# One more block's output in seven half-size products, and one unit transposed by DMA instead of TensorE

## The chip, the cores and the metric

The kernel runs on one core of one Trainium2 chip. The metric is the device time of one execution in microseconds. In the profile, PE is TensorE's matmuls, PEld its weight loads, DVE is VectorE, ACT is ScalarE, POOL is GpSimd, SP (SyncE) the engine that issues the DMAs. The granted clock is the share of TensorE's full clock that it was allowed to run at; 1.0 is all of it.

## The reference

Attention in chunks of 64 tokens, then a bilinear feed-forward layer:

```python
# q, k, v: (8, 8, 576, 64); w_a, w_b: (512, 1536); w_out: (1536, 512)
scores = q_c @ k_c.T / sqrt(64)            # in each chunk of 64 tokens
attn   = softmax(scores);  out = attn @ v_c
x = out.transpose(0, 2, 1, 3).reshape(4608, 512)
return ((x @ w_a) * (x @ w_b)) @ w_out     # float32 (4608, 512)
```

## The kernel before

The 4608 tokens are 9 blocks (0 to 8) of 512, and each block is 2 units of 256. For a unit, q and k are loaded, cast to bf16 on GpSimd (unit 0's on VectorE), transposed, multiplied to scores, normalized, and multiplied with v to give `xT`. Then a block goes through the two feed-forward products (`ab`) and the output product.

From block 2 on, products are done by a seven-product scheme for 2x2 block matrices (Strassen-Winograd): seven half-size products in place of eight, at the price of sums. For the output the sums are `s1..s4` of the activations `ab` and `t1..t4` of the weights `w_out`. `combine_wo` and `combine_ab` make them, all on GpSimd:

```python
def combine_wo(part, j):                   # weight sums, third j of the rows of w_out
    ...
    o, x0, x1, op = ((t3, b22, b12, SUB), (t2, t3, b11, ADD),
                     (t4, b21, t2, SUB), (t1, b12, b11, SUB))[part]
    nc.gpsimd.tensor_tensor(out=o, in0=x0, in1=x1, op=op)

def combine_ab(K, part, j, eng=None):      # sums of block K's activations
    ...
    o, x0, x1, op = ((s1, a21, a22, ADD), (s2, s1, a11, SUB),
                     (a21, a11, a21, SUB), (s4, a12, s2, SUB))[part]
    (eng or nc.gpsimd).tensor_tensor(out=o, in0=x0, in1=x1, op=op)
```

Blocks 0 and 1 are different. While they run, attention still has to get ahead and the weights are still being summed. Block 0 is done plainly; block 1 plainly in two halves, `h(1)` being one step of it; and both outputs are plain products (`out_part`, matmuls of 512 columns). Every engine works through its own list in program order. The code that builds the lists:

```python
cast(4); cast(5); load(6)                  # units 0 to 5 are transposed on PE (PE_UNITS = 6)
...                                        # block 1, interleaved with attention:
bring(6); h(8); out_0(0); transpose_pe(4); h(2); scores(4); out_0(1); transpose_pe(5)
h(1); normalize(4); h(1); scores(5); h(1); values(4); bring(7); h(1)
normalize(5); out_0(2); values(5); combine_x(2); h(1); out_0(3)

for K in range(2, NBLK):
    for i in range(NWP):                   # group i of block K
        ...
        now.p1()
        if last: last.add7()               # VectorE: two additions, of C and u, v
        chunk(...)                         # a part of the previous block's output
        if last: last.p3()
        attend(K, i, 0); now.p6()
        if last: last.p4()                 # PE: product t4 into C, after add7
        ...
```

`bring(U)` casts unit U, loads the next one and transposes U by DMA. `add7` comes first in VectorE's list for each group, and PE cannot start product `p4` before it. Whatever stands in VectorE's list ahead of `add7` can stall PE.

The softmax here doesn't subtract the row's maximum and nothing guards it: scores larger than these inputs give would overflow.

Of the kernel before, what the change touches and what calls it, by code (L numbers as in the profile page):

```python
# [8 lines left out]


PE_UNITS = 6
AB_SCALE = 256.0
OUT_SCALE = 1.0 / AB_SCALE

# [2 lines left out]
def kernel(  # L17
# [10 lines left out]
    nc = tc.nc  # L28
# [48 lines left out]
    warm_in = consts.tile([128, 512], BF16)  # L77
# [33 lines left out]
    def cast_ab(i):  # L111
        for n in ("wb", "wa"):
            w_ab[n, i] = wpool.tile([128, NKT, WCOL], FP16, name=f"{n}{i}")
            nc.gpsimd.tensor_copy(out=w_ab[n, i], in_=staged.pop((n, i)))
# [31 lines left out]
            out=wo_sb[:, 2 * i:2 * i + 2], in_=staged.pop(("wo", i))  # L146
        )

    def combine_wo(part, j):
        k = slice(2 * j, 2 * j + 2)  # L150
        k2 = slice(HFT + 2 * j, HFT + 2 * j + 2)
        b11, b12 = wo_sb[:, k, 0:256], wo_sb[:, k, 256:512]
        b21, b22 = wo_sb[:, k2, 0:256], wo_sb[:, k2, 256:512]
        t1, t2, t3, t4 = [t[:, k] for t in wo_t]
        o, x0, x1, op = (
            (t3, b22, b12, SUB), (t2, t3, b11, ADD), (t4, b21, t2, SUB), (t1, b12, b11, SUB)
        )[part]
        nc.gpsimd.tensor_tensor(out=o, in0=x0, in1=x1, op=op)

    raw = {}  # L160

# [19 lines left out]
    def load(U, names="qkv"):  # L181

        for n in names if U < NU else "":
            src = {"q": q, "k": k, "v": v}[n]
            if U < PE_UNITS and n != "v":
                st = st_pool.tile([128, H, 2, D], FP32, name="st")
                for r, b, s, m in pieces(U):
                    nc.sync.dma_start(
                        out=st[r // 2:(r + m) // 2].rearrange("p h i d -> p h (i d)"),
                        in_=src[b, :, s:s + m, :].rearrange("h (p i) d -> p h (i d)", i=2),  # L190
                    )
                staged[n, U] = st.rearrange("p h i d -> p i h d")
            else:
                staged[n, U] = st_pool.tile([128, 2, H, D], FP32, name="st")
                load_natural(staged[n, U], src, U)

    def cast(U, names="qkv"):
        for n in names if U < NU else "":
            raw[n, U] = raw_pool.tile(
                [128, 2, H, D], BF16, name=f"{n}_raw"  # L200
            )
            eng = nc.vector if U == 0 and n != "v" else nc.gpsimd
            eng.tensor_copy(out=raw[n, U], in_=staged.pop((n, U)))  # L203


# [2 lines left out]
    def transpose_pe(U, names="qk"):  # L208
        if U not in qkt:
            qkt[U] = qkt_pool.tile([128, 2, 2, NKT, 128], BF16, name="qkt")  # L210
        for n in names:
            w = "qk".index(n)
            src = raw.pop((n, U))
            tp = bank().bitcast(BF16).rearrange("c (i m p) -> c i m p", i=2, m=NKT)
            for i in range(2):
                for m in range(NKT):
                    nc.tensor.transpose(
                        tp[:, i, m, :],
                        src[:, i, 2 * m:2 * m + 2, :].rearrange("p j d -> p (j d)"),
                        identity,  # L220
                    )
            dst = qkt[U][:, w].rearrange("c g m (p i) -> c i m g p", i=2)
            for i in range(2):
                cp = nc.vector.tensor_copy if w == 0 or U == 1 else nc.scalar.copy
                cp(out=dst[:, i], in_=tp[:, i].rearrange("c m (g p) -> c m g p", g=2))

    def transpose_dma(U):
# [12 lines left out]
    def scores(U):  # L240
        t = qkt.pop(U)
        E_of[U] = sm_pool.tile([128, 2, NKT, 2, 64], BF16, name="E")
        sc = [bank().rearrange("p (m g s) -> p m g s", m=NKT, g=2) for _ in range(2)]
        for m in range(NKT):
            for g in range(2):
                for j in range(2):
                    for cl in range(2):
                        nc.tensor.matmul(
                            sc[j][cl * 64:cl * 64 + 64, m, g, :],
                            t[j * 64:j * 64 + 64, 1, g, m, cl * 64:cl * 64 + 64],  # L250
                            t[j * 64:j * 64 + 64, 0, g, m, cl * 64:cl * 64 + 64],
                            start=True,
                            stop=True,
                        )
        for j in range(2):
            nc.scalar.activation(out=E_of[U][:, j], in_=sc[j], func=AF.Exp, scale=scale)
# [55 lines left out]
    def slot(s=None, f=None):  # L312

        if s is not None and s >= NU:
            s = None
        if f is not None:
            sums(f)
            inverse(f)
        if s is not None:
            scores(s)  # L320
        if f is not None:
            values(f)

    def bring(U):

        if U >= NU:
            return
        cast(U, "qk")
        load(U + 1, "q")
        if U < NU:  # L330
            transpose_dma(U)
        cast(U, "v")
        load(U + 1, "kv")
# [285 lines left out]
    with tc.manual_schedule(  # L619
# [22 lines left out]
        cast_ab(1)  # L642
        cast_ab(2)
        cast_ab(3)
        transpose_pe(1, "q")
        scores(0)
        transpose_pe(1, "k")
        sums(0, halves=None)
        keep_warm(2)
# [30 lines left out]
        for ft in range(NFT):  # L680
            ab_step(0, ft)
            if 3 <= ft < 10:
                combo()
            if ft == 6:
                transpose_pe(2)
            if ft == 8:
                slot(2)
            if ft == 10:
                slot(None, 2)

        cast(4)
        cast(5)
        load(6)

        outs = []

# [4 lines left out]
        def half(ft, u):  # L701
            ab_step(1, ft, 256 * u, 256 * u + 256)
            if ft > 9 if u == 0 else ft != 5 and ft != 9 and ft != 11:
                combo()
            if u == 1 and ft % 2 and ft > 2:
                combine_w(ft // 2 - 1, 3)

        halves = [(ft, u) for u in range(2) for ft in range(NFT)]

# [19 lines left out]
        h(2)  # L729
        values(3)  # L730
        bring(6)
        h(8)
        out_0(0)
        transpose_pe(4)
        h(2)
        scores(4)
        out_0(1)
        transpose_pe(5)
        h(1)
        normalize(4)  # L740
        h(1)
# [1 line left out]
        h(1)  # L743
        values(4)
        bring(7)
        h(1)
        spread[:] = [psum_a, psum_q]
        normalize(5)
        out_0(2)
        spread[:] = [psum_t]  # L750
        values(5)
        combine_x(2)
        h(1)
        out_0(3)
        assert not halves and not combos

# [21 lines left out]
        def attend(K, i, n):  # L778
            for f in attention.get((K, i, n), ()):
                f()  # L780

        wo_sums = [(p, j) for p in range(4) for j in range(3)]
        last = None
        chunks = {
            2: (0, 0, 1, 1, 1, 1, 1, 1, 1, 1, 1, 1),
            3: (1, 1, 2, 2, 1, 1, 2, 2, 1, 1, 1, 1),
            4: (1, 1, 1, 1, 1, 1, 2, 2, 1, 1, 1, 1),
            NBLK - 1: (1,) * 12,
        }
# [8 lines left out]
        for K in range(2, NBLK):  # L798
            for i in range(NWP):
                if i == 1:  # L800
                    if K == 2:
                        outs += [
                            lambda tg=tg, p=p: out_part(1, tg, p, (psum_o, psum_q)[tg % 2])
                            for tg in range(4) for p in range(3)
                        ]
                    else:
                        for j in range(3):
                            combine_ab(K - 1, 3, j)
                if i in (1, 3):
                    bring(2 * K + 4 if i == 1 else 2 * K + 5)  # L810
                if K == 2:
                    for _ in range(2 if i < 3 else 1):
                        combine_wo(*wo_sums.pop(0))
                if K == 3 and i == 1:
                    while wo_sums:
                        combine_wo(*wo_sums.pop(0))
                if K == 2 and i == 0:
                    combine_w(NWP - 1, 3)
                if K > 2 and i == 0:
                    g = OutGroup(K - 1)  # L820
                    outs += [
                        lambda g=g, n=n, th=th: g.part(n, th) for n in range(7) for th in range(2)
                    ]
                now = Group(K, i)
                now.p1()
                if last:
                    last.add7()
                chunk(chunks.get(K, chunks[4])[2 * i])
                if last:
                    last.p3()  # L830
                attend(K, i, 0)
                now.p6()
                if last:
                    last.p4()
                    finish(last)
                now.p2()
                chunk(chunks.get(K, chunks[4])[2 * i + 1])
                attend(K, i, 1)
                now.p5()
                now.p7()  # L840
                last = now
# [47 lines left out]
```

## Time and profile before

| | before |
|---|---|
| median time | 310.88 us (310.45 to 311.45) |
| span in the profile | 309.1 us |
| PE busy | 95% |
| GpSimd busy | 58% |

The page of the kernel before: the busy table, and rows of the table of 40 slices (7.7 us each, busy share in tenths).

```profile
PE 293.2 (95%) x3476; PEld 228.9 (74%) x3478; DVE 205.2 (66%) x342; ACT 194.0 (63%) x350; POOL 178.6 (58%) x168
...
PE   2879989999999999999999999999999999999995
...
POOL 0575656644538688936782777377737711780560
PEclk9999999999999999999999999999999999999999
```

PE is the limit. After the start its row is 9 nearly everywhere. GpSimd has room: 178.6 us busy of 309.

The view of what PE waited for (total us, times, longest):

```profile
PE pb L355 <- DVE xT L305: 1.7, 1, 1.7
PE pa L355 <- DVE xT L305: 1.5, 1, 1.5
PE pa L263 <- ACT v_sb L363: 0.5, 1, 0.5
```

Apart from the waits for the first casts (5.4, 0.8 and 0.5 us) these are the longest. Nothing after the start of block 1 is over 0.5 us. GpSimd's timeline around the end of block 1 (start us, us, engine, line, operation, output<-input, count, and idle time before it with what ended it):

```profile
64.36 1.04 POOL L203 CAST v_raw<-st 128x1024 bf16<-128x1024 f32 x1 [0.78 <-PE pt L217]
67.44 1.31 POOL L203 CAST q_raw<-st 128x1024 bf16<-128x1024 f32 x1 [2.04 <-DMA st<-in_q_dram]
69.98 1.04 POOL L203 CAST k_raw<-st 128x1024 bf16<-128x1024 f32 x1 [1.23 <-DMA st<-in_k_dram]
...
79.36 1.04 POOL L203 CAST k_raw<-st 128x1024 bf16<-128x1024 f32 x1 [4.29 <-DMA st<-in_k_dram]
...
95.37 3.37 POOL L158 TENSOR_TENSOR wot<-wot,wo 128x512 f16<-128x512 f16 x3
```

GpSimd idles for the DMA here, up to 4.3 us at a time. Three of its sums take 3.37 us (the last line). VectorE and PE at the start of block 2:

```profile
81.41 0.43 DVE L385 TENSOR_TENSOR s<-s,xT 128x512 f16<-128x512 f16 x1
...
87.67 0.69 DVE L443 TENSOR_TENSOR c_sb<-pc,v_sb 128x512 f32<-128x512 f32 x1 [1.74 <-ACT v_sb L416]
88.28 0.69 DVE L444 TENSOR_TENSOR pc<-pc,u_sb 128x512 f32<-128x512 f32 x1
```

```profile
88.34 0.60 PE L405 MATMUL pb<-s,t 128*128 128x256 f16 x4
89.02 0.60 PE L405 MATMUL pc<-xT,t 128*128 128x256 f16 x4
```

A VectorE sum (128x512, 16 bit) takes 0.43 us here. The two additions end at 88.97 us, and the `p4` product (`pc<-xT,t`) starts at 89.02 us.

### The profile page before, as it was taken

What the parts mean: (1) busy time and instruction counts of PE and PEld (TensorE: products, weight loads), DVE (VectorE), ACT (ScalarE), POOL (GpSimd) and SP (SyncE); (2) the same over time, 40 slices, a digit from 0 to 9 for tenths busy, and PEclk for the clock granted to TensorE, in tenths of its full rate; (3) what the DMA queues carried; (4) which work ended last, traced back from release to release, by engine and by line L of the source; (5) the groups of instructions that cost most, each with busy time, mean ns of one, the idle gap of its engine ahead of it and who ended that gap; (6) DMA issues with size and microseconds to landing.
All of it is one profiled execution on the core that took longest, in us unless ns stands there. A gap on an engine that the chain in (4) does not pass through costs nothing.

```text
span 309.1 us, 8485 instructions
## 1 busy us (share of the span) xinstructions
PE 293.2 (95%) x3476; PEld 228.9 (74%) x3478; DVE 205.2 (66%) x342; ACT 194.0 (63%) x350; POOL 178.6 (58%) x168
## 2 busy tenths in 40 slices
PE   2879989999999999999999999999999999999995
PEld 1534557866566768888888888888888888888884
DVE  3345663967866686567757776677668766965872
ACT  1643557448575657766877686768775867566531
POOL 0575656644538688936782777377737711780560
PEclk9999999999999999999999999999999999999999
DMA  7999999999989994698439943993493000300025
GB/s 233 303 382 279 274 326 344 246 228 200 272 209 221 222 240 120 91 251 220 125 70 244 241 130 86 215 293 94 102 174 134 6 0 2 136 3 3 0 77 197
DMA packets 138887, 54.03 MB, mean 175 GB/s; under 512 B 114016, under 2 KB 132960, under 8 KB 138848
## 3 DMA queue, kind: packets, MB, share of 16 engines
q1 hardware_dynamic: 138704, 53.36, 70.8%
q8 instruction: 27, 0.44, 0.6%
q10 hardware_dynamic: 144, 0.13, 0.1%
q14 instruction: 12, 0.10, 0.1%
HBM read 37.75 MB, written 9.44 MB: 153 GB/s over the span
## 4 chain that ended last, share of the span: by engine, by line
PE 81%; DVE 6%; ACT 4%; POOL 4%; issue 2%; DMA 2%; SPq 0%; DVEq 0%; POOLq 0%; ACTq 0%
PE pb L405 17%; PE pc L405 11%; PE pa L405 10%; PE po L541 9%; PE pq L541 8%; PE pb L609 3%; PE pb L355 3%; PE pc L355 3%; PE po L355 3%; DMA st<-in_q_dram 2%; PE pq L355 2%; POOL so L485 2%; PE pa L355 2%; PE pt L296 1%; PE pt L263 1%
## 5 line engine op out<-in xcount | busy, mean ns | idle before, releaser
L405 PEld LDWEIGHTS <-t 128*128 128x128 f16 x504 | 48.3, 98 | 9.9 <-issue 3.9
L443 DVE TENSOR_TENSOR c_sb<-pc,v_sb 128x512 f32<-128x512 f32 x42 | 28.8, 686 | 35.7 <-ACT v_sb L416 35.0
L485 POOL TENSOR_TENSOR so<-ab_sb 128x512 f16<-128x512 f16 x20 | 23.1, 1152 | 50.9 <-DVE ab_sb L455 50.9
L405 PE MATMUL pb<-s,wa 128*128 128x256 f16 x336 | 50.6, 273 | 0.1
L405 PE MATMUL pa<-xT,wb 128*128 128x256 f16 x336 | 50.4, 273 | 0.0
L416 ACT COPY u_sb<-pb 128x512 f32<-128x512 f32 x42 | 24.7, 587 | 24.8 <-PE pb L405 23.5
L541 PEld LDWEIGHTS <-ab_sb 128*128 128x128 f16 x336 | 32.9, 98 | 4.2 <-issue 0.4
L405 PEld LDWEIGHTS <-wb 128*128 128x128 f16 x336 | 32.9, 98 | 4.0
L405 PEld LDWEIGHTS <-wa 128*128 128x128 f16 x336 | 31.0, 98 | 6.2 <-issue 0.2
L203 POOL CAST k_raw<-st 128x1024 bf16<-128x1024 f32 x17 | 18.1, 1062 | 28.8 <-DMA st<-in_k_dram 28.8
L455 DVE SCALAR_TENSOR_TENSOR ab_sb<-pc,c_sb 128x512 f16<-128x512 f32 x42 | 28.9, 688 | 6.9 <-PE pc L405 5.5
L455 DVE SCALAR_TENSOR_TENSOR ab_sb<-pb,b_sb 128x512 f16<-128x512 f32 x42 | 28.8, 687 | 2.8 <-PE pb L405 2.4
L416 ACT COPY v_sb<-pb 128x512 f32<-128x512 f32 x42 | 24.9, 592 | 8.1 <-PE pb L405 8.1
L423 ACT COPY pb<-pa 128x512 f32<-128x512 f32 x42 | 24.6, 586 | 8.4 <-PE pa L405 8.3
L416 ACT COPY b_sb<-pa 128x512 f32<-128x512 f32 x42 | 25.0, 595 | 7.7 <-PE pa L405 7.7
L444 DVE TENSOR_TENSOR pc<-pc,u_sb 128x512 f32<-128x512 f32 x42 | 29.0, 689 | 0.0
L203 POOL CAST v_raw<-st 128x1024 bf16<-128x1024 f32 x18 | 19.2, 1065 | 15.6 <-DMA st<-in_v_dram 9.3
L305 DVE TENSOR_TENSOR xT<-pt,ln 128x512 f16<-128x512 f32 x30 | 19.4, 684 | 12.2 <-PE pt L296 12.2
L541 PEld LDWEIGHTS <-so 128*128 128x128 f16 x252 | 24.6, 98 | 3.4 <-issue 0.5
L203 POOL CAST q_raw<-st 128x1024 bf16<-128x1024 f32 x17 | 17.9, 1056 | 13.4 <-DMA st<-in_q_dram 12.8
L405 PE MATMUL pb<-s,t 128*128 128x256 f16 x168 | 25.3, 273 | 0.4 <-ACT pb L423 0.4
L405 PE MATMUL pc<-s,t 128*128 128x256 f16 x168 | 25.2, 272 | 0.5 <-DVE ab_sb L455 0.5
(132 smaller groups left out, 578.9 us busy)
## 6 DMA issues: line engine op xcount, KB each, us to landing
out_dram<-o_sb SPq DMA_DIRECT2D x34, 256.0 KB, 3.4
st<-in_v_dram SPq DMA_DIRECT2D x32, 256.0 KB, 4.2
st<-in_q_dram SPq DMA_DIRECT2D x23, 256.0 KB, 4.8
st<-in_k_dram SPq DMA_DIRECT2D x23, 256.0 KB, 3.5
st<-in_moe_w_b_dram SPq DMA_DIRECT2D x6, 512.0 KB, 8.0
st<-in_moe_w_a_dram SPq DMA_DIRECT2D x6, 512.0 KB, 8.0
st<-in_moe_w_out_dram SPq DMA_DIRECT2D x6, 512.0 KB, 6.7
st<-in_q_dram SPq DMA_DIRECT2D x4, 512.0 KB, 5.6
```

The costliest lines, as they stand in the source:

```text
L203: eng.tensor_copy(out=raw[n, U], in_=staged.pop((n, U)))
L305: nc.vector.tensor_tensor(out=x.rearrange("p m (g c s) -> p m g c s", g=2, c=2)[:, :, :, cl, :], in0=av[cl], in1=rs[:, cl].rearrange("p m ...
L355: nc.tensor.matmul(ps[n], w_ab[n, i][:, kt, o:o + 128], xT[:, kt, c0:c1], start=(kt == 0), stop=(kt == NKT - 1),)
L405: nc.tensor.matmul(t[:, h * 256:h * 256 + 256], w[:, kt, h * 128:h * 128 + 128], x[:, kt], start=start and h == 0 and kt == 0, stop=h == 1 ...
L416: nc.scalar.copy(out=t, in_=src)
L423: nc.scalar.copy(out=self.B, in_=self.A)
L443: nc.vector.tensor_tensor(out=self.c, in0=self.C, in1=self.v, op=ADD)
L444: nc.vector.tensor_tensor(out=self.C, in0=self.C, in1=self.u, op=ADD)
L455: nc.vector.scalar_tensor_tensor(out=self.dst[:, :, c0:c0 + 256], in0=t.rearrange("p (h n) -> p h n", h=2), scalar=AB_SCALE, in1=o.rearran ...
L485: (eng or nc.gpsimd).tensor_tensor(out=o, in0=x0, in1=x1, op=op)
L541: nc.tensor.matmul(t[:, c0:c0 + 256], a[:, kt, th * 128:th * 128 + 128], w[:, kt], start=n in (0, 4) and first and kt == 0, stop=last and ...
L609: nc.tensor.matmul(out_ps[K, tg], ab_tiles[K][:, ft, tg * 128:tg * 128 + 128], wo_sb[:, ft], start=(ft == 0), stop=(ft == NFT - 1),)
```

## The change

The intent: block 1's output in seven products as well, which spares PE work; unit 5 transposed by DMA (`PE_UNITS = 5`, `bring(5)`), which spares PE its 16 transposes; and smaller moves at the start. The sums that this needs are brought forward: `t3, t2, t4` and block 1's `s1, s2, s3` to GpSimd during block 1, and `t1` and `s4` to VectorE at the start of group 1 of block 2, ahead of its `add7`.

```diff
-PE_UNITS = 6
+PE_UNITS = 5
@@ cast
-            eng = nc.vector if U == 0 and n != "v" else nc.gpsimd
+            eng = nc.vector if (n, U) in (("q", 0), ("k", 0), ("k", 1)) else nc.gpsimd
@@ transpose_pe: evictions
-                cp = nc.vector.tensor_copy if w == 0 or U == 1 else nc.scalar.copy
+                dve = i == 0 if U == 0 or (U, w) == (1, 0) else w == 0 or U == 1
+                cp = nc.vector.tensor_copy if dve else nc.scalar.copy
@@ start
+        scores(0)
         transpose_pe(1, "q")
-        scores(0)
@@ block 0
+            if ft == 9:
+                sums(2)
+                inverse(2)
             if ft == 10:
-                slot(None, 2)
+                values(2)
@@ block 1
+        def combine_wo_all(part, eng=None):
+            for j in range(3):
+                combine_wo(part, j, eng)
         cast(4)
-        cast(5)
-        load(6)
+        bring(5)
+        combine_wo_all(0)
@@ half
+            if u == 1 and ft % 2 and ft > 6:
+                for part in range(3):
+                    combine_ab(1, part, ft // 2 - 3)
@@
         bring(6)
+        combine_wo_all(1)
@@
-        transpose_pe(5)
@@
         bring(7)
+        combine_wo_all(2)
         h(1)
-        spread[:] = [psum_a, psum_q]
+        spread[:] = [psum_q, psum_o]
         normalize(5)
@@
+        whole = bank(psum_q)
+        nc.tensor.matmul(whole, warm_in[:, :128], warm_in, start=True, stop=True)
         out_0(3)
@@ blocks 2 to 8: parts of the previous block's output in each half group
-            2: (0, 0, 1, 1, 1, 1, 1, 1, 1, 1, 1, 1),
-            3: (1, 1, 2, 2, 1, 1, 2, 2, 1, 1, 1, 1),
@@
                 if i == 1:
                     if K == 2:
-                        outs += [... out_part(1, tg, p, ...) ...]   # cut
-                    else:
-                        for j in range(3):
-                            combine_ab(K - 1, 3, j)
+                        combine_wo_all(3, nc.vector)
+                    for j in range(3):
+                        combine_ab(K - 1, 3, j, nc.vector if K == 2 else None)
-                (the weight sums spread over blocks 2 and 3)
-                if K > 2 and i == 0:
+                if i == 0:
                     g = OutGroup(K - 1)
```

More of the change, by code (lines that the diff above doesn't have):

```diff
@@ L147, in cast_wo, with combine_wo @@
         )
-    def combine_wo(part, j):
+    def combine_wo(part, j, eng=None):
         k = slice(2 * j, 2 * j + 2)
@@ L157, in combine_wo @@
         )[part]
-        nc.gpsimd.tensor_tensor(out=o, in0=x0, in1=x1, op=op)
+        (eng or nc.gpsimd).tensor_tensor(out=o, in0=x0, in1=x1, op=op)
     raw = {}
@@ L780, in attend @@
                 f()
-        wo_sums = [(p, j) for p in range(4) for j in range(3)]
         last = None
         chunks = {
[2 rows of a table removed]
             4: (1, 1, 1, 1, 1, 1, 2, 2, 1, 1, 1, 1),
@@ L801 @@
                     if K == 2:
-                        outs += [
-                            lambda tg=tg, p=p: out_part(1, tg, p, (psum_o, psum_q)[tg % 2])
-                            for tg in range(4) for p in range(3)
-                        ]
-                    else:
-                        for j in range(3):
-                            combine_ab(K - 1, 3, j)
+                        combine_wo_all(3, nc.vector)
+                    for j in range(3):
+                        combine_ab(K - 1, 3, j, nc.vector if K == 2 else None)
                 if i in (1, 3):
                     bring(2 * K + 4 if i == 1 else 2 * K + 5)
-                if K == 2:
-                    for _ in range(2 if i < 3 else 1):
-                        combine_wo(*wo_sums.pop(0))
-                if K == 3 and i == 1:
-                    while wo_sums:
-                        combine_wo(*wo_sums.pop(0))
                 if K == 2 and i == 0:
                     combine_w(NWP - 1, 3)
-                if K > 2 and i == 0:
+                if i == 0:
                     g = OutGroup(K - 1)
```

## The prediction

> **What bounds the kernel now.** TensorE: busy 95% of the 309.1 us span (busy table), 81% of the last chain. From 136 us on the windows show it busy almost without a gap; only the first 136 us can give much back. It waits there (view of waits) 5.4 us for the first cast, 0.8 and 0.5 for unit 1's casts, 1.7 at 17.1 us (unit 1's xT), 1.5 at 42.0 us (unit 2's xT), 0.5 at 75.5 us (bank of the sums of unit 5), 0.4 at 84 us, 0.3 at 131 us (GpSimd's output-weight sums).
>
> **What TensorE saves.**
> - Block 1's output: 48 matmuls of 512 columns (12 groups of 0.86 us) become 84 of 256 columns (14 groups of 0.655 us): -1.2.
> - Unit 5's 16 PE transposes (69.45 to 70.34 us): -0.9.
> - Prologue (split evictions, scores(0) earlier, unit 1's k cast on VectorE, 0.69 against 1.04 us): -0.6.
> - Unit 2's sums one step earlier, but ScalarE's b_sb copy then sits behind ln and exp (2.1 us): -0.5 of the 1.5 us.
> - Other banks for sums(5): -0.5; waits at 84 and 131 us: -0.5.
> - New whole-bank matmul that waits for the last copy: +0.3.
> Sum -3.9 us.
>
> **What it costs.** GpSimd becomes the limit for about 25 us. After unit 5's v cast (ends 65.4 us before), its in-order queue now holds, ahead of block 1's s2: 9 weight sums (10.2 us), 8 ab sums (9.2 us; 1.15 us per 128x512 op), 6 casts (6.2 us) = 25.6 us. So s2's last third comes at 91.0 us. VectorE's s4 needs it, and sits in VectorE's order before the first additions of block 2 (87.67 us before), which the t4 product (89.02 us before) needs. TensorE wants that product at about 87.5 us; it gets it at 91.0 + 0.4 + 1.4 = 92.8 at best: a stall of at least 5 us.
>
> The DMA makes it worse: its busy share is about 1 up to 115 us. Unit 5's q and k now load in 256 B runs, not 512 B, and two transposes are added (landing 2.7 us alone, 3.4 to 5.3 typical). The Trainium skill, "DMA: Bandwidth & Descriptors", section "Why small descriptors are slow (HBM only)", gives a fixed overhead per packet; this trace agrees in direction: 303 to 382 GB/s in slices of longer runs, about 200 to 270 where 256 B runs dominate. I estimate 4 to 5 us more DMA time, so unit 6's k and v reach their casts 3 to 4 us later and GpSimd idles. Stall then 5 to 9 us; net of what it absorbs, 6.3.
>
> **Prediction.** 310.9 - 3.9 + 6.3 = about 313.3 us; 309.5 to 317.0. Faster by over 2%: 0.04; within 2%: 0.87; slower by over 2%: 0.09.
>
> **What would show it.** One TensorE stall of 4 to 9 us in block 2's second group (86 to 96 us), its wait on VectorE's additions, VectorE's on GpSimd's "so"; GpSimd near 100% busy from 65 to 95 us; unit 6's k cast at 73 us or later (69.98 before). Gains: block 0 starts at 18.3 us (18.87); the wait before block 1 about 1 us; unit 5's transposes gone. After 136 us: no change.
>
> **What would make it wrong.** If s2 is ready in time (sums faster, or VectorE not held in order), the time falls to about 307. If unit 5's transposes land after 71 us, scores(5) stalls too, partly hidden in the later stall.

## The result

The changed kernel takes 322.3 us (median of 4, 321.07 to 322.93) against 310.88 us: slower, ratio 1.0361, 95% interval 1.0323 to 1.0400. A ratio is the mean time of one kernel's runs over that of the other's runs of the same rounds, so it is not quite the ratio of the medians. Executions over 1.5% slower than the fastest of the same kernel are left out of the means. Run again later beside other kernels it took 322.51 us against 310.54 us (ratio 1.0366). The predicted 313.3 us and its range, 309.5 to 317.0 us, were too low.

The page of the changed kernel, the same rows (slices of 8.0 us). Line numbers above 220 are one higher than before.

```profile
PE 294.7 (92%) x3497; PEld 232.6 (73%) x3499; DVE 214.6 (67%) x345; ACT 197.1 (62%) x354; POOL 185.4 (58%) x173
...
PE   2779999999763999999999999999999999999995
...
POOL 1465665576999207864695559357916730781460
PEclk9999999999985999999999999999999999999999
```

PE's row falls to 7, 6 and 3 in the slices from 80 to 104 us, where GpSimd's row is at 9, and the granted clock falls in the same place. What PE waited for:

```profile
PE pc L406 <- DVE pc L445: 7.7, 1, 7.7
PE po L542 <- DVE ab_sb L365: 2.4, 1, 2.4
PE pa L356 <- DVE xT L306: 0.6, 1, 0.6
```

Two new waits: 7.7 us of the `p4` product for VectorE's addition, and 2.4 us before it. The wait of 0.5 us at the sums of unit 5 is gone, and the one before block 1 fell from 1.5 to 0.6 us. GpSimd now:

```profile
66.43 1.04 POOL L203 CAST v_raw<-st 128x1024 bf16<-128x1024 f32 x1 [2.05 <-DMA st<-in_v_dram]
67.43 3.73 POOL L158 TENSOR_TENSOR wot<-wo 128x512 f16<-128x512 f16 x3
...
73.81 1.17 POOL L203 CAST k_raw<-st 128x1024 bf16<-128x1024 f32 x1 [1.48 <-DMA st<-in_k_dram]
...
88.47 1.23 POOL L203 CAST q_raw<-st 128x1024 bf16<-128x1024 f32 x1
...
92.02 3.72 POOL L158 TENSOR_TENSOR wot<-wo,wot 128x512 f16<-128x512 f16 x3
...
96.92 1.15 POOL L486 TENSOR_TENSOR so<-so,ab_sb 128x512 f16<-128x512 f16 x1
```

From 66.43 us to the last `s2` sum (`so<-so,ab_sb`, 96.92 to 98.07 us) it idles for data only 2.7 us. Three sums now take 3.7 us and a cast 1.23 us (1.04 undisturbed). VectorE and PE:

```profile
79.97 1.07 DVE L386 TENSOR_TENSOR s<-xT 128x512 f16<-128x512 f16 x1
81.08 1.26 DVE L386 TENSOR_TENSOR s<-s,xT 128x512 f16<-128x512 f16 x1
...
87.43 3.72 DVE L158 TENSOR_TENSOR wo<-wo 128x512 f16<-128x512 f16 x3
91.07 2.55 DVE L486 TENSOR_TENSOR so<-ab_sb,so 128x512 f16<-128x512 f16 x2
98.10 1.35 DVE L486 TENSOR_TENSOR so<-ab_sb,so 128x512 f16<-128x512 f16 x1 [4.48 <-POOL so L486]
99.38 0.68 DVE L444 TENSOR_TENSOR c_sb<-pc,v_sb 128x512 f32<-128x512 f32 x1
99.98 0.68 DVE L445 TENSOR_TENSOR pc<-pc,u_sb 128x512 f32<-128x512 f32 x1
```

```profile
92.39 0.60 PE L406 MATMUL pb<-s,t 128*128 128x256 f16 x4
100.71 1.01 PE L406 MATMUL pc<-xT,t 128*128 128x256 f16 x4 [7.72 <-DVE pc L445]
101.52 1.06 PE L406 MATMUL pa<-xT,wb 128*128 128x256 f16 x4
```

VectorE finishes the second of its three `s4` sums at 93.6 us, idles 4.48 us for GpSimd's `s2`, and only then gets to the additions. The `p4` product starts at 100.71 us, 11.7 us later than before. The sums with two SBUF operands take 1.1 to 1.4 us each, not 0.42. After the stall, a group of four matmuls takes 0.81 us from start to next start (100.71 to 101.52), where it took 0.44 before: half speed. From `p4` to the end the changed kernel needs 218.6 us (319.3 - 100.71), the one before 220.1 us (309.1 - 89.02). So the loss lies wholly ahead of `p4`, and 1.5 us come back after it. The mark does not part equal work, though: in the changed kernel three of the 14 parts of block 1's output (2.0 us) stand ahead of it, in the one before one of 12 (0.86 us). About 1.1 us of what comes back is therefore work that only moved ahead of the mark.

My theory (A) was now this: GpSimd's in-order list holds `s2` back, and VectorE's order passes that on to PE. Rival B: the added DMA work of unit 5 is the cause. Rival C: VectorE is too slow by itself, because its sums collide with GpSimd's. A further suspect was the clock.

### The profile page after: what moved, and what is told of

Read it like the earlier page. It is cut to its first block, busy times and chain, and to the rows that moved or that the text cites. A ratio compares the mean times of both kernels' runs of the same rounds, so it can differ in the third digit from the quotient of the medians.

```text
span 319.3 us, 8542 instructions
## 1 busy us (share of the span) xinstructions
PE 294.7 (92%) x3497; PEld 232.6 (73%) x3499; DVE 214.6 (67%) x345; ACT 197.1 (62%) x354; POOL 185.4 (58%) x173
## 4 chain that ended last, share of the span: by engine, by line
PE 75%; POOL 7%; DVE 5%; DMA 4%; ACT 3%; issue 2%; SPq 2%; POOLq 0%; ACTq 0%; DVEq 0%
PE pb L406 18%; PE pc L406 12%; PE pa L406 11%; PE po L542 11%; PE pq L542 9%; DMA st<-in_v_dram 3%; PE pb L356 3%; POOL wot L158 2%; POOL so L486 2%; PE pc L356 2%; PE po L356 2%; SPq L176 2%; DMA st<-in_k_dram 2%; PE pt L297 1%; PE pt L264 1%
## 5 line engine op out<-in xcount | busy, mean ns | idle before, releaser
L486 POOL TENSOR_TENSOR so<-ab_sb 128x512 f16<-128x512 f16 x23 | 26.9, 1167 | 56.5 <-DVE ab_sb L456 56.5
L406 PE MATMUL pa<-xT,wb 128*128 128x256 f16 x336 | 51.3, 276 | 0.0
L542 PEld LDWEIGHTS <-ab_sb 128*128 128x128 f16 x384 | 38.2, 99 | 7.9 <-issue 2.9
L406 PE MATMUL pc<-xT,t 128*128 128x256 f16 x168 | 25.6, 275 | 7.7 <-DVE pc L445 7.7
L203 POOL CAST k_raw<-st 128x1024 bf16<-128x1024 f32 x16 | 17.1, 1067 | 25.9 <-DMA st<-in_k_dram 24.8
L542 PEld LDWEIGHTS <-so 128*128 128x128 f16 x288 | 28.1, 98 | 3.4
L486 POOL TENSOR_TENSOR so<-so,ab_sb 128x512 f16<-128x512 f16 x23 | 26.7, 1161 | 1.8
L486 POOL TENSOR_TENSOR ab_sb<-ab_sb 128x512 f16<-128x512 f16 x23 | 26.9, 1172 | 0.0
```

The lines of the kernel that those rows point to most:

```text
L203: eng.tensor_copy(out=raw[n, U], in_=staged.pop((n, U)))
L406: nc.tensor.matmul(t[:, h * 256:h * 256 + 256], w[:, kt, h * 128:h * 128 + 128], x[:, kt], start=start and h == 0 and kt == 0, stop=h == 1 ...
L542: nc.tensor.matmul(t[:, c0:c0 + 256], a[:, kt, th * 128:th * 128 + 128], w[:, kt], start=n in (0, 4) and first and kt == 0, stop=last and ...
```

## The experiments

Twelve runs followed, one of them (e0) of the changed kernel again, each timed against the kernel before on its own chip. Not all ran on the same chip, so where two experiments are compared it is by their ratios.

| run | what it is | median us | before beside it | ratio (95%) |
|---|---|---|---|---|
| e0_after_again | changed kernel | 322.51 | 310.54 | 1.0366 (1.0338 to 1.0393) |
| e1_dma_only | before + unit 5 by DMA | 312.74 | 310.63 | 1.0072 (1.0052 to 1.0093) |
| e2_seven_only | changed, unit 5 on PE | 318.47 | 310.63 | 1.0244 (1.0222 to 1.0266) |
| e3_start_only | before + the start's moves | 310.49 | 310.63 | 0.9997 (0.9974 to 1.0019) |
| e4_s2_first | changed, `s2` ahead of `t4` | 318.50 | 310.63 | 1.0247 (1.0231 to 1.0264) |
| e5_warm | changed + 33 filler matmuls | 321.45 | 311.34 | 1.0334 (1.0272 to 1.0396) |
| e5b_warm | changed + 38 filler matmuls | 320.39 | 310.54 | 1.0304 (1.0280 to 1.0329) |
| e6_no_s2_wait | changed, `s4` without `s2` (wrong result) | 317.12 | 311.34 | 1.0185 (1.0151 to 1.0219) |
| e9_small_sums | changed, sums cut (wrong result) | 311.96 | 311.34 | 1.0024 (0.9985 to 1.0063) |
| e10_memsets | changed, memsets for sums (wrong result) | 321.28 | 311.20 | 1.0341 (1.0306 to 1.0376) |
| e7_late | changed, mended order | 314.55 | 311.34 | 1.0101 (1.0040 to 1.0162) |
| e8_mended | mended, unit 5 on PE | 309.51 | 310.54 | 0.9959 (0.9937 to 0.9982) |

### The parts of the change alone

**e1_dma_only**, the kernel before with the DMA part:

```diff
-PE_UNITS = 6
+PE_UNITS = 5
-        cast(5)
-        load(6)
+        bring(5)
-        transpose_pe(5)
```

> The kernel before with only unit 5 moved to DMA transposes (natural 256 B loads, brought in with its two transposes; no PE transposes). Theory A (GpSimd's in-order queue of block 1's sums is the cause): near the kernel before, 309.5 to 311.5 us (0.9 us of PE transposes saved, DMA a little later), no stall over 2 us at the start of block 2. Rival B (the added DMA work is the cause): 316 us or more.

Measured 312.74 us, ratio 1.0072. Rival B falls as the main cause: the DMA part alone costs 0.7%, not 3.6%. But it is more than theory A allowed. In this trace the start of block 2 has no long stall. The `p4` product itself is not late (87.78 us, 89.02 before). The loss shows at 112.7 and 118.8 us, where PE waits 1.1 and 0.7 us for VectorE's multiplication. There GpSimd's sums of block 2, shifted by the later casts, lie on top of four of VectorE's sums of `xT`, which take 1.12 to 1.37 us instead of 0.42 (0.46, 1.26, 0.82 and 0.41 us in the kernel before). So by this trace the later DMA acts here through a collision of the two engines, which the prediction does not reckon with; no run tests that by itself.

**e2_seven_only**, the changed kernel with unit 5 back on PE:

```diff
-PE_UNITS = 5
+PE_UNITS = 6
-        bring(5)
+        cast(5)
+        load(6)
         out_0(1)
+        transpose_pe(5)
```

> The changed kernel with unit 5 back on PE transposes (all else of the change kept). Theory A: the stall stays, shorter by the 3 to 4 us in which GpSimd waited for late data of units 5 and 6: 317 to 320 us, and the last s2 sum ends at 94 to 96 us (98.1 in the changed kernel). Rival B: 308 to 311 us.

Measured 318.47 us, ratio 1.0244; the last `s2` sum ended at 95.1 us, and the longest wait was still 5.6 us. As theory A expected. Of the 3.6% loss, 1.2% goes with the DMA part (1.0361 against 1.0244, or about 3.6 us), and the trace says how: without the late data unit 5's v cast ends at 65.7 us (67.47), GpSimd waits 1.3 us for data (2.7), and `s2` ends 3.0 us earlier. It costs more here than alone (0.7%).

**e3_start_only**, the kernel before with the moves at the start (split evictions, k cast of unit 1 on VectorE, scores(0) first, unit 2's sums one step earlier; the diff is that of the change).

> The kernel before with only the changes to the start: evictions of units 0 and 1 split over two engines, unit 1's k cast on VectorE, scores(0) first, unit 2's sums one step earlier. My prediction gave 1.1 us of gain (about 309.8). The trace of the changed kernel says the two evictions run one after the other (ScalarE waits for VectorE's half), so the start loses 0.4 us and only the wait before block 1 shrinks (1.5 to 0.6 us): 310.4 us, within 0.5 of the kernel before.

Measured 310.49 us, ratio 0.9997: nothing. Block 0 starts at 18.95 us (18.87 before), because ScalarE's half of the eviction waits for VectorE's half and the two run one after the other. The wait before block 1 does fall to 0.6 us, but that gain is gone by the end.

### GpSimd's list and VectorE's order

**e4_s2_first**, the changed kernel with one reordering:

```diff
         bring(7)
-        combine_wo_all(2)
         h(1)
@@
         h(1)
+        combine_wo_all(2)
         whole = bank(psum_q)
```

> The changed kernel with one reordering in GpSimd's queue: the three t4 weight sums (3.7 us, needed only by the last product of block 1's output) go behind the last three ab sums of block 1 instead of ahead of them. Theory A: s2 is ready 3.7 us earlier, the long stall of block 2 falls from 7.7 to about 4 us, the time falls by 3 to 4 us to about 318.5. If the stall has another cause (rival C: VectorE itself too slow after its own delays), no change within 1 us.

Measured 318.50 us, ratio 1.0247, a gain of 1.1% (about 3.6 us), as expected in time. The long wait fell only to 6.8 us in the profiled run, and not to 4, because PE reached it earlier too. VectorE's third `s4` sum still waits for `s2`:

```profile
95.55 1.35 DVE L486 TENSOR_TENSOR so<-ab_sb,so 128x512 f16<-128x512 f16 x1 [2.27 <-POOL so L486]
```

`s2` ended at 95.5 us (98.1 in the changed kernel), and the `p4` product started at 98.16 us (100.71). By the times, three sums (3.7 us) taken out of the list ahead of `s2` gave back their own length; by the two profiled runs, 2.6 us of it. The list is on the critical path.

**e6_no_s2_wait**, the changed kernel with other data in `s4` for block 1, so that VectorE waits for no GpSimd sum (wrong result):

```diff
-            (s1, a21, a22, ADD), (s2, s1, a11, SUB), (a21, a11, a21, SUB), (s4, a12, s2, SUB)
+            (s1, a21, a22, ADD), (s2, s1, a11, SUB), (a21, a11, a21, SUB),
+            (s4, a12, a22 if K == 1 else s2, SUB)
```

> The changed kernel with VectorE's three s4 sums for block 1 reading other data than s2 (wrong result on purpose), so VectorE waits for no GpSimd sum. If GpSimd's queue alone makes the stall: the product starts at about 89 us and the time falls to 311 or less. Theory with contention: VectorE's 12 sums with two SBUF operands still take 1.2 to 1.4 us each beside GpSimd's sums (0.42 alone), so its list still ends only at about 95 us, the product starts at 96 to 97 us and the time is 317 to 319 us.

Measured 317.12 us, ratio 1.0185. VectorE in this run:

```profile
87.54 3.84 DVE L158 TENSOR_TENSOR wo<-wo 128x512 f16<-128x512 f16 x3
91.31 3.72 DVE L487 TENSOR_TENSOR so<-ab_sb 128x512 f16<-128x512 f16 x3
95.55 0.68 DVE L445 TENSOR_TENSOR pc<-pc,u_sb 128x512 f32<-128x512 f32 x1
```

No wait is left, yet the additions end only at 96.2 us, and PE still waits 4.5 us. So there are two limits, one close behind the other: GpSimd's list (98.1 us in the changed kernel), and behind it VectorE's own list, stretched from about 5 us (12 sums of 0.42) to 15 us. Taking away the first alone saves 1.8%.

**e10_memsets**, the changed kernel with each of the 18 brought-forward GpSimd sums replaced by memsets of the same output, which read nothing (wrong result):

```diff
+            nc.gpsimd.memset(o, 0.0)
+            nc.gpsimd.memset(o, 0.0)
+            nc.gpsimd.memset(o[:, :, 0:64], 0.0)
-        (eng or nc.gpsimd).tensor_tensor(out=o, in0=x0, in1=x1, op=op)
```

> The changed kernel with each of GpSimd's 18 sums (weights, block 1) replaced by three memsets of the same output, about 1.2 us together by an estimate from the 0.2 us of the 128x128 memset in the trace (wrong result on purpose): GpSimd stays occupied for about as long but reads nothing from SBUF meanwhile. Theory (VectorE's two-operand sums and GpSimd's reads exclude each other): VectorE's first sums of block 2 take 0.42 us each beside the memsets (still up to 1.2 beside a cast), the 2.4 us stall before the scores disappears, and GpSimd's list is 2 to 3 us shorter; the long stall stays, ending 2 to 4 us earlier: 317.5 to 320 us. If VectorE's sums still take 1.3 us, occupancy of GpSimd by itself slows VectorE and my reading of the contention falls.

Measured 321.28 us, ratio 1.0341. GpSimd and VectorE in this run:

```profile
80.41 0.52 POOL L161 MEMSET wot<- 128x512 f16 x1
...
82.30 0.52 POOL L497 MEMSET so<- 128x512 f16 x1
```

```profile
80.17 0.42 DVE L393 TENSOR_TENSOR s<-s,xT 128x512 f16<-128x512 f16 x1
82.18 1.09 DVE L159 TENSOR_TENSOR wo<-wo 128x512 f16<-128x512 f16 x3
...
99.17 0.42 DVE L494 TENSOR_TENSOR so<-ab_sb,so 128x512 f16<-128x512 f16 x1 [10.39 <-POOL so L498]
```

This separates the two. GpSimd is as occupied as before (three memsets take 1.31 us, a contended sum took 1.22 to 1.33), but VectorE's sums are back at 0.42 us and the 2.4 us wait is gone. So it is not GpSimd's being busy that slows VectorE, but its reading of SBUF. The Trainium skill says just this, "SBUF — State Buffer", section "Who interferes with whom": a VectorE instruction with two SBUF inputs contends with a GpSimd instruction that reads SBUF, not with one that only writes it. The trace agrees, with 0.42 us beside memsets and 1.26 to 1.37 us beside sums. The time, however, did not fall to what I expected (317.5 to 320 us), and the intervals of 1.0341 here and 1.0361 for the changed kernel overlap: the three memsets are as long as a contended sum, the list is no shorter, VectorE now idles 10.39 us for `s2`, and PE waits 11.9 us. In the changed kernel VectorE's slowness by itself is hidden behind GpSimd's list. Rival C is real, but second in line.

**e9_small_sums**, the changed kernel with the same 18 sums cut to an eighth of their columns (the rest zeroed at the start; wrong result):

```diff
+        c = slice(0, 32 if K == 1 and not eng else 256)      # combine_ab; combine_wo alike
-        (eng or nc.gpsimd).tensor_tensor(out=o, in0=x0, in1=x1, op=op)
+        (eng or nc.gpsimd).tensor_tensor(out=o[:, :, c], in0=x0[:, :, c], in1=x1[:, :, c], op=op)
```

> The changed kernel with the 18 GpSimd sums of the output weights and of block 1 cut to an eighth of their columns (wrong result on purpose; everything else, the waits too, kept). Theory: both the queue and the contention go, VectorE's sums at the start of block 2 fall back from 1.3 to about 0.42 us each, the long stall and the 2.4 us one before it vanish, 308 to 311 us (unit 5's DMA still costs 2). If VectorE's sums stay at 1.3 us, the contention is not with GpSimd's sums.

Measured 311.96 us, ratio 1.0024: nearly the whole loss is the sums', by both roads together. The expectation (308 to 311 us, no long stall) missed by 1 us. In the profiled run, the slowest of the five (314.62 us), a wait of 3.1 us was left, since unit 7's v cast waited for the DMA until 89.9 us and stood ahead of `s2` in the list. The order, with late data in it, is enough to stall PE even when the sums cost almost nothing. VectorE's sums of `xT` took 0.42 to 0.53 us there.

### The clock

**e5_warm** and **e5b_warm**, the changed kernel with filler for PE just ahead of the stalled product (the second with 38):

```diff
+                    if (K, i) == (2, 1):
+                        t = bank(psum_t)
+                        for _ in range(33):
+                            nc.tensor.matmul(t, warm_in[:, :128], warm_in, start=True, stop=True)
                     last.p4()
```

> The changed kernel with 33 idle matmuls of 512 columns (about 7 us, into a spare bank) put on TensorE just ahead of the product that stalls, so that it works through the stall and does no more than wait otherwise. Theory: after the stall TensorE ran about 3.4 us at roughly half speed (granted clock 0.62 in that window), so this gives back 1.3 to 1.7 us: about 320.7 us, with the window after the stall at a clock near 1.0 and the stalled product still starting near 100.7 us. If the low clock costs nothing: unchanged at 322.3.

> The changed kernel with 38 idle matmuls (about 8.2 us) just ahead of the stalled product; the run with 33 was 0.9 us faster than the changed kernel measured on another chip, within their scatter, and its filler ended 2.8 us before the product in the profiled run. Theory: clock after the stall near 1.0 (mean 0.99 or more) and 1.0 to 1.7 us faster than the changed kernel beside it. If the low clock costs nothing, equal within 0.4 us.

The first was inconclusive: 321.45 us with a scatter of 4.4 us, on another chip than the changed kernel, and in its profiled run the filler ended before the product could start. The second, beside the changed kernel on one chip, measured 320.39 against 322.51 us, so 2.1 us faster (1.0 to 1.7 expected). The product in the changed kernel beside it, and PE in this run:

```profile
101.89 1.01 PE L406 MATMUL pc<-xT,t 128*128 128x256 f16 x4 [8.87 <-DVE pc L445]
```

```profile
93.27 8.37 PE L839 MATMUL pt<-warm_in 128*128 128x512 bf16 x38
101.47 0.60 PE L407 MATMUL pc<-xT,t 128*128 128x256 f16 x4
101.90 0.60 PE L407 MATMUL pa<-xT,wb 128*128 128x256 f16 x4
```

The product starts at 101.47 us (101.89 without the filler), and the group after it follows in 0.43 us, not 0.81. The mean granted clock is 0.994 to 1.0 against 0.979 to 0.984. From the product to the end it is 217.1 us against 219.0. So about 2 us of the loss are the slow clock after the stall, not the stall itself. The Trainium skill, "TensorE: Matmul & The Clock Gate", section "What's actually happening", says that an idle array falls to half its clock and that it takes some 3.4 us of activity to come back. The traces agree roughly: the granted clock was 0.5 for 3.1 us after the product's start at 100.71 us in the first profile of the changed kernel, and for 4.2 us after 101.89 us in that of e0. Half of 4.2 is an estimate of 2.1 us lost, as much as the filler gave back.

### A mended version

**e7_late**, the changed kernel with nothing of block 1's activation sums on VectorE:

```diff
-                        combine_ab(K - 1, 3, j, nc.vector if K == 2 else None)
+                        combine_ab(K - 1, 3, j)
-                    if K == 2:
-                        combine_wo_all(3, nc.vector)
+                if K == 2 and i < 3:
+                    combine_wo(3, i, nc.vector)
         chunks = {
+            2: (0, 0, 1, 1, 1, 1, 2, 2, 2, 2, 1, 1),      # block 1's output starts one group later
```

> The changed kernel mended without touching GpSimd's sums of blocks 1: s4 of block 1 goes to GpSimd as in the later blocks, the t1 weight sums are spread one per group over VectorE, and block 1's seven products start one group later and are bunched in groups 3 and 4. Theory: VectorE no longer waits for GpSimd ahead of the additions, s2 (at about 96 us) is ready when its product comes, no stall over 2 us: 310.5 to 313.5 us, what is left over the kernel before being unit 5's DMA (2.1 us) and contention. If a stall of 5 us stays, the order on VectorE was not the cause.

Measured 314.55 us, ratio 1.0101, with a wide scatter (312.32 to 316.75). The order was the cause of the long stall, but the expectation missed by 1 us. A wait of 2.7 us stays at the same product, where none over 2 us was expected (VectorE's sums, contended, now end at 91.2 us), and 1.0 and 1.1 us more come at 119.8 and 125.9 us, where block 2's own GpSimd sums are now late and collide again.

**e8_mended** also puts unit 5 back on PE (as e2) and the start as before, keeping unit 2's sums one step earlier, and moves `t4`, `t1` and `s4` behind `s2` on GpSimd:

```diff
-        combine_wo_all(2)                   # after bring(7)
         out_0(3)
+        combine_wo_all(3)                   # t1, on GpSimd
+                if (K, i) == (2, 2):
+                    combine_wo_all(2)
+                    for j in range(3):
+                        combine_ab(1, 3, j)
         chunks = {
+            2: (0, 0, 1, 1, 1, 1, 1, 1, 2, 2, 2, 2),
```

> Seven products for block 1's output kept, unit 5 on PE transposes, the start as before (unit 2's sums earlier kept); VectorE gets none of block 1's sums: s4 and the t1 and t4 weight sums go to GpSimd behind s2, and the seven products start one group later and are bunched at the end of block 2. Theory: no wait of the additions for GpSimd, contention left only on VectorE's own sums at 80 to 88 us (about 1 us of stall at most); saved 1.2 (products) + 0.5 (bank) + 0.4 (unit 2): 308.5 to 310.5 us. Over 312 would say that GpSimd cannot carry block 1's sums at all without slowing TensorE.

Measured 309.51 us, ratio 0.9959 (0.9937 to 0.9982), with the right result: faster than both kernels, though than the one before by only 0.4%, clear of noise. The waits left inside blocks 1 and 2, the longest first:

```profile
PE pc L355 <- DVE ab_sb L364: 0.4, 1, 0.4
...
PE pb L405 <- ACT pb L423: 0.4, 1, 0.4
...
PE pc L405 <- DVE pc L444: 0.2, 1, 0.2
```

VectorE's sums are still contended here (0.93 to 1.37 us), and `p4` starts at 90.44 us, but PE waits for the addition only 0.2 us. The sums did not get cheaper; they got out of the way. Several things changed at once here, so the nearest comparison is with e2, which also has unit 5 on PE: 1.0244 there, 0.9959 here, with the start worth nothing (e3).

## Why the prediction was wrong

**Right:** the place and the mechanism. The predicted stall came in block 2's second group, at the named product, through VectorE's additions and GpSimd's "so"; e2, e4 and e6 bear it out. Unit 6's k cast came at 73.81 us (predicted: 73 or later). After the stall 1.5 us come back, although the slow clock costs about 2 there. Unit 5's PE transposes and the 0.5 us wait are gone. GpSimd was 86% busy from 65 to 95 us, where "near 100%" was predicted.

**The step that failed is the size of one term: "at 91.0 + 0.4 + 1.4 = 92.8 at best: a stall of at least 5 us", with its upper bounds "5 to 9 us" and net 6.3.** I added 6.3 us for a PE that would want the product at 87.5 us, which puts its start at 93.8 us. It started at 100.71 us, 13.2 us after 87.5. PE's own wait, 7.7 us, does lie within "5 to 9 us", but by luck: PE too came late, at 93.0 us (100.71 - 7.72), since a wait of 2.4 us that I had not foreseen, a stretch at half clock after it, and two more parts of block 1's output stood ahead. Against the best case of 92.8 us, the product started 7.9 us later:

| piece | predicted at best | measured | difference |
|---|---|---|---|
| unit 5's v cast ends | 65.4 | 67.47 | +2.1 |
| GpSimd waits for data until `s2` | 0 | 2.7 | +2.7 |
| GpSimd's work until `s2` | 25.6 | 27.9 | +2.3 |
| from `s2` to the product | 1.8 | 2.6 | +0.8 |

The third row is 98.07 - 67.47 - 2.7. The first two rows are late data, 4.8 us. Unit 6's own delay was foreseen well: its k and v reached their casts 3.8 and 3.9 us later than before (3 to 4 predicted). But the list without waits would be ready for unit 6's v at 70.9 us (65.4, then 3.4 for three sums and 2.1 for two casts), and even before the change v came only at 72.3. So by an estimate from these numbers a delay of 3 to 4 us makes a wait of 4.4 to 5.4 us, which I had not added up. The first row also varies: unit 5's v cast began at 65.7 to 67.0 us in five profiles of this list, and at 67.5 to 69.8 us in the four taken on the chip of e6.

The section of the Trainium skill that the prediction cites, "Why small descriptors are slow (HBM only)" in "DMA: Bandwidth & Descriptors", gives a cost per packet, so it bears on the short runs alone. No run here separates these from the two added transposes. SyncE's list, first before, then with the change, shows a cause that the prediction does not name, the order of issue:

```profile
64.11 2.87 SPq L176 DMA_DIRECT2D st<-in_k_dram  x3
```

```profile
65.94 1.33 SPq L231 DMA_TRANSPOSE qkt<-q_raw  x1
...
68.68 1.96 SPq L176 DMA_DIRECT2D st<-in_k_dram  x3
```

Unit 6's k is issued 4.6 us later. For 2.7 us of that, unit 5's two transposes stand ahead of it in SyncE's list; the other 1.8 us are there already when unit 6's q has been issued.

The last two rows of the table are the collision of GpSimd and VectorE on SBUF reads. The prediction has no term for it: it counts 1.15 us for every GpSimd sum and 0.4 us for VectorE's `s4`, as they last in a trace where the two engines seldom sum at the same time. The same trace already had a few sums of VectorE at 1.26 us, under a GpSimd sum or cast (`s<-xT,s` at 82.09 us, for one). VectorE's 12 sums took 15 us in place of 5.

**A term was missing:** the clock. A stall that long costs again when it ends, about 2 us by e5b.

**One gain was not there:** "Prologue ... -0.6" measured 0 (e3). Block 0 started at 19.23 us, not 18.3.

**A gain ahead of a wait whose end another engine sets is worth nothing here.** The savings before `p4` (unit 5, the banks, unit 2) could only make PE arrive earlier at a product whose start GpSimd's list decided. I counted this right for the best case, but it is why no saving could soften the loss.

Left open: how the 3.6% divides exactly between list and collision. The two stretch each other, since a contended GpSimd sum is also a longer list, and e6, e9 and e10 change more than one of them at a time. What they show is an order: the list first, VectorE's stretched sums next, with additions that would end 4.5 us earlier (96.2 us in e6, 100.7 in the changed kernel).

## What to carry to other kernels

When work is moved to an engine with idle time, add up its whole in-order list up to the first result that the critical engine needs, including the waits for data inside it, and look at what stands behind that result in the next engine's list. Sums of two SBUF operands on VectorE and GpSimd at the same time were not parallel here: plan them apart, or count VectorE's sums as three times as long and GpSimd's as nearly a fifth longer, as measured here. The version that won (e8) put the less urgent sums behind the urgent result and left their cost as it was.

## What the Trainium skill lacked or had wrong

- "SBUF — State Buffer", "Who interferes with whom", names the contention and says that the second to issue blocks. Its sizes (VectorE 6.8 times slower, GpSimd 1.5 times) are for one order of issue or the other. In a steady mix here VectorE's two-operand sum of 128x512 went from 0.42 to 1.26 to 1.37 us beside GpSimd's sums or casts, and GpSimd's sum only from 1.15 to 1.33 us and its cast from 1.04 to 1.23 us. VectorE loses a factor of three, GpSimd nearly a fifth.
- "TensorE: Matmul & The Clock Gate", "What's actually happening", puts the fall to half clock after an idle window of about 3.4 us. In the changed kernel a recorded wait of 2.4 us (to 85.31 us) was already followed by groups of four matmuls that took 0.85 us instead of 0.44, with a clock of 0.68 over the window from 85 to 90 us. The length of the wait alone does not decide it: after one of 2.16 us in e5_warm the clock fell to 0.5, after one of 2.17 us in e6_no_s2_wait it stayed at 1.00.
